# Attention and feed-forward on one core: feed-forward groups of 384 tokens behind three groups of 256, one PSUM bank for the inner units, one set of score operands

## The chip, the cores and the metric

The kernel runs on one core of one Trainium2 chip. A core has a matrix engine (TensorE, here PE, with its weight loads as PEld), VectorE (DVE), ScalarE (ACT), GpSimd (POOL), and SyncE (SP), which here issues every DMA. Work memory is SBUF; matmuls write to PSUM, which has 8 banks, each of 512 float32 numbers for each of 128 partitions. The metric is the device time of one execution in microseconds (us), lower is better.

## The reference

64 heads (8 batches of 8) of causal attention with a decay, each over 576 positions of width 64, then a two-layer feed-forward over all 4608 tokens (512 to 2048 to 512):

```python
scores = scale * q @ k.T;  decay = cum[:, None] - cum[None, :]     # cum = cumsum(log f)
scores = where(causal, -1e9, scores + decay)
attn = softmax(scores);  x = attn @ v                              # per head
x = x.transpose(0, 2, 1, 3).reshape(4608, 512)                     # heads side by side
h = x @ w_in;  g = maximum(0.01 * h, h);  out = g @ w_out
```

## The kernel before, in words

All large products are made with operands that are split in a high and a low part, and a product is the sum of three matmuls: high by high, high by low, low by high. So the feed-forward needs, for each block of 128 inner units and each group of tokens, 4 (pieces of 512 inputs) x 3 = 12 matmuls for `h`, and 3 matmuls for each 128 tokens for the second layer (`o`).

The program has three stages. In the first (about 166 us) the first 256 positions of three batches are attended to ("early" heads, two at a time: tiles `sce`, `ze`, `tre`, `pte`, `ave`), while the weights come in and are split (tiles `wraw`, `wt`, `win_h`, `win_l`, `wout_h`, `wout_l`) by ACT and DVE. These 768 tokens are feed-forward groups 0, 1 and 2. In the second stage 64 tasks, one for each head, run as a pipeline: in the step of task t stand the scores of t (`sc`, into the exponentials `z`), the transposes of t-1 (`tr`, into the high and low parts `ph`, `pl`), the products with the values of t-1 (`av`, added up by ACT's `y` and DVE's `x`), a normalisation for each pair of heads (`rb`), and `split(t+1)`, which makes the score operands of the next task. The third stage is feed-forward alone (from about 1143 us).

A score is two accumulating matmuls, one with operands `s1`, `m1`, one with `s2`, `m2`. `split` makes them: ACT copies q and k (lines 320, 321), POOL subtracts the high part (line 129, a helper) into half of `s1` and half of `m2`, and three DMAs bring half of `s1` and the decay into `s2` and `m2` (lines 322 to 324). Before, there are two buffers of `s1` and `m1`, and two fixed tiles each of `s2` and `m2` (`s2a`, `s2b`, `m2a`, `m2b`) that even and odd tasks use in turn.

The feed-forward is a generator, `ffn`, that is advanced in quanta: between the pieces of a task stands `fill(step)`, which lets some quanta pass. Before, groups are 256 tokens, and a pair of 128-unit blocks is made in one PSUM bank (tag `h`, two banks): quanta are 12 matmuls of the first block, 12 of the second, and then 6 `o` matmuls for each 128 tokens of the pair before. After the second block ACT applies the activation over 512 columns (line 512, tile `g`), and DVE makes the high and low parts `gh` and `gl` (lines 515, 516). Accumulators of the second layer have one bank each, `o0` and `o1`; two banks each belong to tags `sc` and `tr`: 8 in all. A group's inputs `xs` come by one DMA (line 472) when the group before is partly done, and are split by DVE and POOL (lines 477, 129). At the end of a group ACT copies `o` to `ost` (two buffers, line 551) and SP stores it (line 553). The number of quanta of a task follows from the quanta that are ready, at most `MAXQ`, in eighths of it for each `fill`.

A scheduler places the instructions on each engine's queue; an engine works through its queue in that order. The order is the one that the program's rows show below.

```python
step = min(have / (left + SLACK), MAXQ) / 8
```

Of the kernel before, what the change touches and what calls it, by code (L numbers as in the profile page):

```python
# [20 lines left out]
MAXQ = 9  # L21
# [15 lines left out]
def forgetting_attention_ffn(ctx, tc, qT, kT, v4, vr, f, w_in, w_out, out):  # L37
# [18 lines left out]
    NG = NTOK // T  # L56
    NQ = NFC // 2 * (2 + T // P)
# [42 lines left out]
    def warm(n):  # L100

        ps = psum.tile([P, 512], F32, tag="h", name=f"warm_{len(warmed)}")
# [93 lines left out]
    for name, tag, x, to in (("fck", "s1", fc, dec_k), ("fcq", "m1", start, dec_q)):  # L196
        r = one.tile([P, S], F32R, tag=tag, name=name, bufs=2)
# [40 lines left out]
    def early_scores(b, g):  # L238
# [3 lines left out]
        for o in range(2):  # L242
            s = b * HPB + 2 * g + o
            for i in range(2):
# [9 lines left out]
                z = e[c] = one.tile(  # L254
                    [P, n], F32, tag=tag, name=f"ze_{b}_{g}_{c}", bufs=BUFS.get(tag, 1)
                )
# [14 lines left out]
    def early_values(b, g):  # L271
        e = early[b, g]
        out = psum.tile([P, 512], F32, tag="tr", name=f"ave_{b}_{g}")
        for o in range(2):
# [5 lines left out]
            pt = one.tile([P, 3 * P], F32, tag=("z4", "m2a")[o], name=f"pte_{b}_{g}_{o}")  # L280
# [9 lines left out]
        xh, xl = groups[b]  # L290
# [5 lines left out]
    def fix():  # L296

        for x in "ab":
            for w, n in (("s2", 2), ("m2", 4)):
                y = fixed[w + x] = one.tile([P, S], F32R, tag=w + x, name=f"fixed_{w}{x}")  # L300
                nc.gpsimd.memset(y[:D].bitcast(F32), 0.0)
                nc.gpsimd.memset(y[:n].bitcast(F32), 1.0)
            y = fixed["sum" + x] = one.tile([P, NCH, 2], F32, tag="sum" + x, name=f"fixed_sum{x}")
            nc.gpsimd.memset(y, 1.0)
# [5 lines left out]
    def split(t):  # L310
# [157 lines left out]

    def fetch_group(n):
        if n not in groups and n not in staged and (n + 1) * T <= ready[0]:  # L470
            xs = staged[n] = one.tile([P, NCC, T], F32R, tag="b4", name=f"xs_{n}", bufs=B4)
            nc.sync.dma_start(xs.bitcast(F32), xd[:, n * T:(n + 1) * T].rearrange("(c p) t -> p c t", p=P))

    def split_group(n):
        xs = staged[n]
        xh = one.tile([P, NCC, T], F32R, tag="b4", name=f"xh_{n}", bufs=B4)
        nc.vector.tensor_copy(xh, xs.bitcast(F32))
        minus(xs, xs.bitcast(F32), xh.bitcast(F32))
        groups[n] = (xh, xs)

    def ffn():
# [4 lines left out]
        for at, (n, p0, p1) in enumerate(order):  # L486
            while (n + 1) * T > ready[0]:
# [7 lines left out]
            acc = [None, None]  # L495
            for p in range(p0, p1):
# [3 lines left out]
                ph = psum.tile([P, 2, T], F32, tag="h", name=f"h_{n}_{p}")  # L500
                for e in range(2):
                    fs = slice(e * P, (e + 1) * P)
                    for c in range(NCC):
                        for x, (w, xx) in enumerate(((win_h[p], xh), (win_h[p], xl), (win_l[p], xh))):
                            nc.tensor.matmul(  # L505
                                ph[:, e, :], w[:, c, fs], xx[:, c, :],
                                start=(c == 0 and x == 0), stop=(c == NCC - 1 and x == 2),
                            )
# [3 lines left out]
                nc.scalar.activation(g, ph, AF.Prelu, alpha=0.01)  # L512
# [152 lines left out]
```

## Time and profile before

| what | value |
|---|---|
| three runs | 1254.18, 1258.46 (median), 1259.77 us |
| the profiled execution | span 1251.0 us from the first to the last instruction; no other time of it is on record |
| PE busy, weight loads | 1228.7 us (98%), 1079.2 us (86%) |
| DVE, ACT, POOL busy | 739.0, 609.5, 324.7 us |
| granted PE clock | 1.000 of full speed |
| `h` matmuls, 256 columns | 3456 |
| `o` matmuls, 512 columns | 1728 |
| DMA | 102.49 MB, 82 GB/s on average |

How to read the rows: in a group's row stand line, engine, operation, tiles written and read, shapes and count, then busy time and mean duration, then idle time of the engine just before. A timeline row has the start in us from the span's start, the duration, engine, line and tiles; durations of matmuls overlap, since they are pipelined, so a matmul's price is the time from its start to the next one's. A row of the chain of waits has start, length, and what stood there. A row of the waits view has who waited for whom: us in total, times, longest.

### The profile page before, as it was taken

The page shows a single profiled execution, that of the slowest core. Times are in us where ns is not written, and L with a number is a line of the kernel's source. Part 1 is how long each engine was busy: PE and PEld are TensorE (multiplying, and loading weights), DVE is VectorE, ACT ScalarE, POOL GpSimd, SP SyncE. Part 2 cuts the span into 40 slices and gives each one's busy share as a digit, 9 for nine tenths or more (in the row PEclk, how much of TensorE's full clock was granted, in tenths as well). Part 3 has the DMA queues.
Part 4 walks back from the last instruction along what each step waited for, and adds up shares of the span by engine and source line. Part 5 has one row for each costly group of instructions (what it writes and reads, how often), then busy time and mean ns, then how long its engine had stood idle before and what let it go on. Part 6 is the DMA issues. An engine that isn't in the chain of part 4 may idle for free.

```text
span 1251.0 us, 22163 instructions
## 1 busy us (share of the span) xinstructions
PE 1228.7 (98%) x7964; PEld 1079.2 (86%) x7964; DVE 739.0 (59%) x1837; ACT 609.5 (49%) x1447; POOL 324.7 (26%) x348
## 2 busy tenths in 40 slices
PE   9999999999999999999999999999999999999998
PEld 6667888888998898898988889989999988899997
DVE  7888967766665655655556555453444656764211
ACT  6766556664554554554454445343334545552111
POOL 2000063333233433232223222221322333421000
PEclk9999999999999999999999999999999999999999
DMA  6444342333222322223222222121212222221000
GB/s 196 164 156 145 124 117 89 109 90 96 68 85 84 101 68 59 76 64 96 68 84 85 78 58 64 55 79 43 85 51 66 69 85 75 89 61 42 18 17 18
DMA packets 64078, 102.49 MB, mean 82 GB/s; under 512 B 9057, under 2 KB 32145, under 8 KB 63969
## 3 DMA queue, kind: packets, MB, share of 16 engines
q1 hardware_dynamic: 63968, 101.08, 26.6%
q8 instruction: 63, 1.03, 0.3%
q14 instruction: 47, 0.38, 0.1%
HBM read 74.76 MB, written 18.42 MB: 74 GB/s over the span
## 4 chain that ended last, share of the span: by engine, by line
PE 92%; DVE 3%; DMA 2%; ACT 1%; issue 1%; POOL 0%; SPq 0%; ACTq 0%; DVEq 0%; POOLq 0%
PE h L505 32%; PE o L537 30%; PE sc L352 9%; PE av L421 8%; PE tr L379 7%; PE sce L248 2%; DMA xs<-xd 2%; PE warm L105 1%; PE rb L456 1%; PE ave L283 1%; PE sce L249 1%; DVE gh L515 1%; PE tre L277 1%; DVE fixed_vs L330 0%; ACT g L512 0%
## 5 line engine op out<-in xcount | busy, mean ns | idle before, releaser
L505 PE MATMUL h<-xh,win_h 128*128 128x256 f32 x1152 | 330.8, 287 | 0.1
L505 PE MATMUL h<-xh,win_l 128*128 128x256 f32 x1152 | 326.4, 283 | 0.0
L505 PE MATMUL h<-xs,win_h 128*128 128x256 f32 x1024 | 289.4, 283 | 0.0
L537 PE MATMUL o<-wout_h,gh 128*128 128x512 f32 x576 | 232.4, 404 | 0.2 <-DVE gh L515 0.2
L129 POOL TENSOR_TENSOR s<-qraw,s 64x576 fp32r<-64x576 f32 (+1 forms) x64 | 84.7, 1324 | 566.6 <-ACT s L320 532.2
L537 PE MATMUL o<-wout_l,gh 128*128 128x512 f32 x576 | 226.4, 393 | 0.0
L537 PE MATMUL o<-wout_h,gl 128*128 128x512 f32 x576 | 225.8, 394 | 0.0
L505 PEld LDWEIGHTS h<-xh,win_h 128*128 128x128 f32 x1152 | 219.4, 191 | 4.4 <-ACT xh L291 0.2
L505 PEld LDWEIGHTS h<-xh,win_l 128*128 128x128 f32 x1152 | 219.6, 191 | 0.8 <-issue 0.5
L392 ACT CAST ph<-tr 128x128 fp32r<-128x128 f32 (+3 forms) x272 | 120.1, 444 | 167.3 <-PE tr L379 165.8
L505 PEld LDWEIGHTS h<-xs,win_h 128*128 128x128 f32 x1024 | 195.2, 191 | 3.7
L512 ACT ACTIVATE g<-h 128x512 f32<-128x512 f32 x144 | 85.7, 595 | 228.6 <-PE h L505 223.8
L515 DVE CAST gh<-g 128x512 fp32r<-128x512 f32 x144 | 81.6, 567 | 174.8 <-ACT g L512 172.3
L357 DVE CUSTOM_DVE_ANT_0 z<-sc,tri 128x128 f32<-128x128 f32 (+1 forms) x208 | 107.2, 518 | 122.0 <-PE sc L352 122.0
L363 ACT ACTIVATE z<-z,max 128x128 f32<-128x128 f32 (+1 forms) x208 | 122.5, 589 | 72.9 <-DVE max L357 71.2
L394 DVE TENSOR_TENSOR pl<-tr,ph 128x128 fp32r<-128x128 f32 (+3 forms) x272 | 137.1, 508 | 33.3 <-ACT ph L392 33.2
L537 PEld LDWEIGHTS o<-wout_h,gl 128*128 128x128 f32 x576 | 108.3, 188 | 23.9 <-DVE wraw L162 0.2
L352 PE MATMUL sc<-m,s 128*128 128x128 f32 (+2 forms) x336 | 123.3, 372 | 1.8 <-DVE max L357 1.8
L537 PEld LDWEIGHTS o<-wout_h,gh 128*128 128x128 f32 x576 | 108.8, 189 | 16.0 <-DVE gh L515 0.6
L537 PEld LDWEIGHTS o<-wout_l,gh 128*128 128x128 f32 x576 | 108.8, 189 | 15.3 <-issue 0.2
L516 DVE TENSOR_TENSOR gl<-g,gh 128x512 fp32r<-128x512 f32 x144 | 109.6, 761 | 6.3 <-PE sce L248 2.1
L379 PE MATMUL tr<-ident_r,z 128*128 128x128 f32 x568 | 96.3, 273 | 4.3 <-DVE pl L394 3.0
(113 smaller groups left out, 1836.9 us busy)
## 6 DMA issues: line engine op xcount, KB each, us to landing
kraw<-in_kT SPq DMA_DIRECT2D x128, 144.0 KB
qraw<-in_qT SPq DMA_DIRECT2D x80, 144.0 KB
wraw<-in_w_in SPq DMA_DIRECT2D x16, 512.0 KB
wraw<-in_w_out SPq DMA_DIRECT2D x16, 512.0 KB
vm<-in_v SPq DMA_DIRECT2D x32, 256.0 KB
xs<-xd SPq DMA_DIRECT2D x16, 512.0 KB
out<-ost SPq DMA_DIRECT2D x28, 256.0 KB
xd<-x SPq DMA_DIRECT2D x20, 288.0 KB
```

What stands on the lines that cost most here:

```text
L352: nc.tensor.matmul(ps[:m, :b - a], h["s" + w][:, cols], h["m" + w][:, a:b], start=y == 0, stop=y == 1,)
L357: nc.vector.tensor_tensor_reduce(out=z[:, a:b], in0=ps[:m, :b - a], in1=tri[:m, at:at + b - a], scale=-SCALE, scalar=3.0e38 if x == 0 else ...
L363: nc.scalar.activation(z, z, AF.Exp, bias=h["max"][:m, last:last + 1], scale=-1.0, accum_out=fixed["sum" + "ab"[s // 2 % 2]][:m, i, s % 2: ...
L379: nc.tensor.transpose(ps[:, x * m:(x + 1) * m], z[:m, j * P:(j + 1) * P], ident[:m, :m])
L392: nc.scalar.copy(o, src)
L394: nc.vector.tensor_tensor(o, src, hi.bitcast(F32), op=ALU.subtract)
L421: nc.tensor.matmul(ps[:, a - lo:hi - lo], fixed["vs"][:, odd, j, :], h[w][:, at:at + hi - a], start=(n == 0), stop=(n == len(steps) - 1),)
L505: nc.tensor.matmul(ph[:, e, :], w[:, c, fs], xx[:, c, :], start=(c == 0 and x == 0), stop=(c == NCC - 1 and x == 2),)
L512: nc.scalar.activation(g, ph, AF.Prelu, alpha=0.01)
L515: nc.vector.tensor_copy(gh, g)
L516: nc.vector.tensor_tensor(gl, g, gh.bitcast(F32), op=ALU.subtract)
L537: nc.tensor.matmul(acc[k], gg[:, e, ts], w[:, e, :], start=(fc_ == 2 * p0 and x == 0), stop=(fc_ == 2 * p1 - 1 and x == 2),)
```

## The change

- The first three groups keep 256 tokens; the other 3840 tokens make ten groups of 384 in place of fifteen of 256. Matmuls of `h` have 384 columns there.
- A block of 128 inner units is made by itself: 12 matmuls in one bank, then activation and both parts over 256 or 384 columns. Tag `h` has one bank; the freed bank is `o2`, the accumulator of a group's third 128 tokens.
- A quantum is half of a block: 6 `h` matmuls, or half of the `o` matmuls of the block before (3 or 5 and 4). `MAXQ` goes from 9 to 12, the quanta of the late early steps from 8 to 16.
- There is one buffer of `s1` and of `m1`, and one fixed tile of `s2` and of `m2`. The early heads and the transposed early weights take their scratch tiles from these names.
- `ost` keeps two buffers, for three copies at a group's end.

```diff
-MAXQ = 9
+MAXQ = 12
+LATER = 384
-ZE = (("z0", "z1", "z2", "z3"), ("vm", "s2b", "m2b", "s2a"))
-FQ = (0, 0, 0, 0, 0, 8, 8, 8, 8, 8, 8, 8, 8)
-BUFS = dict(s1=2, m1=2, ost=2)
+ZE = (("z0", "z1", "z2", "z3"), ("vm", "s1", "m1", "s2"))
+FQ = (0, 0, 0, 0, 0, 16, 16, 16, 16, 16, 16, 16, 16)
...
-    NG = NTOK // T
-    NQ = NFC // 2 * (2 + T // P)
+    sizes = [T] * NE + [LATER] * ((NTOK - NE * T) // LATER)
+    first = [sum(sizes[:n]) for n in range(len(sizes))]
+    last = [a + m for a, m in zip(first, sizes)]
+    NG = len(sizes)
+    TM = max(sizes)
+    NQ = NFC * 4
...
-        x = "ab"[t % 2]
-        s1 = h["s1"] = one.tile([P, S], F32R, tag="s1", name=f"s1_{t}", bufs=2)
-        m1 = h["m1"] = one.tile([P, S], F32R, tag="m1", name=f"m1_{t}", bufs=2)
-        s2, m2 = h["s2"], h["m2"] = fixed["s2" + x], fixed["m2" + x]
+        s1 = h["s1"] = one.tile([P, S], F32R, tag="s1", name=f"s1_{t}")
+        m1 = h["m1"] = one.tile([P, S], F32R, tag="m1", name=f"m1_{t}")
+        s2, m2 = h["s2"], h["m2"] = fixed["s2"], fixed["m2"]
...
-            for p in range(p0, p1):
+            for f in range(2 * p0, 2 * p1):
+                p, e = divmod(f, 2)
...
-                ph = psum.tile([P, 2, T], F32, tag="h", name=f"h_{n}_{p}")
-                for e in range(2):
-                    fs = slice(e * P, (e + 1) * P)
...
-                    if e == 0:
+                ph = psum.tile([P, 512], F32, tag="h", name=f"h_{n}_{f}", bufs=1)
+                fs = slice(e * P, (e + 1) * P)
+                mms = [
+                    (a[:, c, fs], b[:, c, :w])
+                    for c in range(NCC)
+                    for a, b in ((win_h[p], xh), (win_h[p], xl), (win_l[p], xh))
+                ]
+                for i, (a, b) in enumerate(mms):
+                    if i == len(mms) // 2:
                         yield True
-                g = one.tile([P, 2, T], F32, tag="b2", name=f"g_{n}_{p}", bufs=B2)
-                nc.scalar.activation(g, ph, AF.Prelu, alpha=0.01)
+                    nc.tensor.matmul(ph[:, :w], a, b, start=i == 0, stop=i == len(mms) - 1)
+                g = one.tile([P, TM], F32, tag="b2", name=f"g_{n}_{f}", bufs=B2)
...
+                nc.scalar.activation(g[:, :w], ph[:, :w], AF.Prelu, alpha=0.01)
+                nc.vector.tensor_copy(gh[:, :w], g[:, :w])
...
-    def second(n, p, p0, p1, gh, gl, acc):
-        for k in range(T // P):
+    def second(n, f, p0, p1, gh, gl, acc):
+        p, e = divmod(f, 2)
+        begin, end = f == 2 * p0, f == 2 * p1 - 1
+        nk = sizes[n] // P
+        done = 0
+        for k in range(nk):
...
+                done += 1
+                if done == (3 * nk + 1) // 2:
+                    yield True
```

Three places of the order show what moves.

PE, first stage, the first blocks of group 0 (`h_<block>`; before, a block's number is that of a pair). Before:

```order
L505 MATMUL h_0_614<-xh_163,win_h_93 128x256
L505 MATMUL h_0_614<-xl_164,win_h_93 128x256
L505 MATMUL h_0_614<-xh_163,win_l_101 128x256
L277 MATMUL tre_3_0_528<-ident_r,ze_3_0_408 128x128
L505 MATMUL h_1_645<-xh_163,win_l_102 128x256
L505 MATMUL h_1_645<-xh_163,win_h_94 128x256
L277 MATMUL tre_3_0_528<-ident_r,ze_3_1_417 128x128 x2
L505 MATMUL h_1_645<-xl_164,win_h_94 128x256
```

With the change, two blocks further on in the same stage:

```order
L519 MATMUL h_3_685<-xl_164,win_h_94 128x256
L519 MATMUL h_3_685<-xh_163,win_l_102 128x256
L552 MATMUL o_0_0_652<-wout_h_110,gh_2_674 128x512
L552 MATMUL o_0_0_652<-wout_l_118,gh_2_674 128x512
L552 MATMUL o_1_0_656<-wout_h_110,gh_2_674 128x512
L552 MATMUL o_1_0_656<-wout_l_118,gh_2_674 128x512
L519 MATMUL h_4_710<-xh_163,win_h_95 128x256
```

Before, matmuls of pair 1 stand on PE while pair 0 is still open in the other bank. Now block 4 begins when block 3 is finished, with four `o` matmuls between them, and its first matmul needs the bank that block 3's activation reads.

ACT, second stage, around `split` (`s_22`, `m_22` are the copies for task 22, `z_20` exponentials of task 20; `fixed_z` holds a task's last exponentials). Before:

```order
L363 ACTIVATE z_20_5353,fixed_suma<-z_20_5353,max_5298 128x512
L512 ACTIVATE g_3_5371<-h_3_5333 128x512
L392 CAST ph_5291<-tr_4_5377 128x5x64
L320 CAST s_22_5652<-qraw_5487 128x576
L321 CAST m_22_5653<-kraw_5490 128x576
L363 ACTIVATE fixed_z_1714,fixed_suma<-fixed_z_1714,max_5298 64x576
L428 COPY y_0_5418<-av_0_5407 64x448
```

With the change:

```order
L364 ACTIVATE z_23_5994,fixed_sumb<-z_23_5994,max_5920 128x512
L393 CAST ph_5913<-tr_4_6012 128x5x64
L321 CAST s_24_6078<-qraw_5881 128x576
L322 CAST m_24_6079<-kraw_5884 128x576
L364 ACTIVATE fixed_z_1812,fixed_sumb<-fixed_z_1812,max_5920 64x576
L429 COPY y_0_6048<-av_0_6037 64x448
```

The copies stand at the same place behind a task's scores, but before they are for the task after next, and now for the next one.

ACT, second stage, at the end of a group (`ost_<k>` is the copy of the k-th 128 tokens). With the change (before, there is no third copy):

```order
L525 ACTIVATE g_0_7030<-h_0_6996 128x384
L429 COPY y_1_7039<-av_1_7036 64x128
L568 COPY ost_0_7045<-o_0_0_6000 128x512
L568 COPY ost_1_7074<-o_1_0_6004 128x512
L568 COPY ost_2_7080<-o_2_0_6008 128x512
L525 ACTIVATE g_1_7106<-h_1_7083 128x384
```

The third copy takes the buffer of the first, so it waits for the first store; the next group's activation `g_1` is queued behind it.

More of the change, by code (lines that the diff above doesn't have):

```diff
@@ L196, in forgetting_attention_ffn @@
     for name, tag, x, to in (("fck", "s1", fc, dec_k), ("fcq", "m1", start, dec_q)):
-        r = one.tile([P, S], F32R, tag=tag, name=name, bufs=2)
+        r = one.tile([P, S], F32R, tag=tag, name=name)
         halves(r, x)
@@ L279, in early_values @@
                 )
-            pt = one.tile([P, 3 * P], F32, tag=("z4", "m2a")[o], name=f"pte_{b}_{g}_{o}")
+            pt = one.tile([P, 3 * P], F32, tag=("z4", "m2")[o], name=f"pte_{b}_{g}_{o}")
             nc.scalar.copy(pt, ps[:, :3 * P])
@@ L289, in early_values @@
             return
-        xh, xl = groups[b]
+        xh, xl = (x[:, :, :T] for x in groups[b])
         nc.scalar.copy(xh[:, g, :], out[:, :T])
@@ L296, in fix @@
     def fix():
+        for w, n in (("s2", 2), ("m2", 4)):
+            y = fixed[w] = one.tile([P, S], F32R, tag=w, name=f"fixed_{w}")
+            nc.gpsimd.memset(y[:D].bitcast(F32), 0.0)
+            nc.gpsimd.memset(y[:n].bitcast(F32), 1.0)
         for x in "ab":
[L299 to L302, printed above, removed]
             y = fixed["sum" + x] = one.tile([P, NCH, 2], F32, tag="sum" + x, name=f"fixed_sum{x}")
@@ L467, in forgetting_attention_ffn, with wide @@
     groups, staged = {}, {}
+    def wide(name, n):
+        return one.tile([P, NCC, TM], F32R, tag="b4", name=f"{name}_{n}", bufs=B4)
     def fetch_group(n):
-        if n not in groups and n not in staged and (n + 1) * T <= ready[0]:
-            xs = staged[n] = one.tile([P, NCC, T], F32R, tag="b4", name=f"xs_{n}", bufs=B4)
-            nc.sync.dma_start(xs.bitcast(F32), xd[:, n * T:(n + 1) * T].rearrange("(c p) t -> p c t", p=P))
+        if n not in groups and n not in staged and last[n] <= ready[0]:
+            xs = staged[n] = wide("xs", n)
+            nc.sync.dma_start(
+                xs[:, :, :sizes[n]].bitcast(F32),
+                xd[:, first[n]:last[n]].rearrange("(c p) t -> p c t", p=P),
+            )
     def split_group(n):
[L475 to L478, printed above, removed]
+        xs, xh = staged[n], wide("xh", n)
+        a, b = (x[:, :, :sizes[n]] for x in (xs, xh))
+        nc.vector.tensor_copy(b, a.bitcast(F32))
+        minus(a, a.bitcast(F32), b.bitcast(F32))
         groups[n] = (xh, xs)
@@ L486, in ffn @@
         for at, (n, p0, p1) in enumerate(order):
-            while (n + 1) * T > ready[0]:
+            w = sizes[n]
+            while last[n] > ready[0]:
                 yield False
@@ L519, in ffn @@
                     yield from second(*pending)
-                if p == p1 - 1 and at + 1 < len(order):
+                if e == 1 and p == p1 - 1 and at + 1 < len(order):
                     m = order[at + 1][0]
@@ L544, in second @@
                 nc.scalar.copy(o, acc[k])
-            elif p == p1 - 1:
+            elif end:
                 if (n, k) in parts:
@@ L551, in second @@
                     nc.scalar.copy(o, acc[k])
-                for x, row, m in segments(n * T // P + k):
+                for x, row, m in segments(first[n] // P + k):
                     nc.sync.dma_start(out[row:row + m, :], o[x:x + m])
-            yield True
+        yield True
     parts = {}
@@ L572, in forgetting_attention_ffn @@
     for n in range(2):
-        groups[n] = tuple(
-            one.tile([P, NCC, T], F32R, tag="b4", name=f"{name}_{n}", bufs=B4)
-            for name in ("xh", "xl")
-        )
+        groups[n] = tuple(wide(name, n) for name in ("xh", "xl"))
     TRI = (NFULL + 1) * P
@@ L605, in forgetting_attention_ffn @@
         now = list(range(*tasks[t][1:])) if t < nt else []
-        have = ready[0] // T * NQ - used[0]
+        have = sum(x <= ready[0] for x in last) * NQ - used[0]
         left = min((e + 2 - t for e in ends if e + 1 >= t), default=1)
```

44 lines of the change are left out of this document (18 added, 26 removed).

## The prediction

> **What bounds the kernel now.** I read the page first (busy shares, the chain of waits), then the stages, then single places in the timeline.
>
> ```profile
> PE 1228.7 (98%) x7964; PEld 1079.2 (86%) x7964; DVE 739.0 (59%) x1837; ACT 609.5 (49%) x1447; POOL 324.7 (26%) x348
> PE 92%; DVE 3%; DMA 2%; ACT 1%; issue 1%; POOL 0%; SPq 0%; ACTq 0%; DVEq 0%; POOLq 0%
> ```
>
> PE is busy for 98% of the span and is 92% of the chain. Where PE's queue has no hole, a matmul less is time saved, and a wait more is time lost. The stages differ in who is next:
>
> ```profile
> 120.00:150.00 30.00, 30.00 (x171) 23.36 (x170) 25.51 (x45) 19.50 (x43) 0.98 (x2) 1.00 0.43 140
> sum 166.00, PE 161.16 PEld 119.03 DVE 136.89 ACT 103.55 POOL 18.30; mean PE 26.86 PEld 19.84 DVE 22.81 ACT 17.26 POOL 3.05
> 900.00:1000.00 100.00, 100.00 (x674) 90.60 (x673) 51.72 (x128) 43.06 (x95) 24.35 (x28) 1.00 0.21 62
> ```
>
> The columns are the window, its length, and then busy time of PE, PEld, DVE, ACT and POOL. Over the first 166 us DVE is at 136.89 (82%) and ACT at 103.55: they have little room there. Late in the second stage DVE is at 52% and ACT at 43%.
>
> **The feed-forward matmuls.** What an `h` and an `o` matmul cost PE is read from the chain in the last stage, where they stand back to back:
>
> ```profile
> 1154.36 2.87 PE h L505 x24
> 1157.23 2.75 PE o L537 x12
> 605.83 0.34 PE L352 MATMUL sc<-fixed_m2b,fixed_s2b 128*128 128x384 f32 x1
> 606.01 0.39 PE L537 MATMUL o<-wout_h,gh 128*128 128x512 f32 x1
> ```
>
> 24 matmuls of 256 columns take 2.87 us, 119.6 ns each; 12 of 512 take 2.75 us, 229.2 ns each. The straight line through both is 10.0 ns for each matmul and 0.428 ns for each column, so 384 columns cost 174.4 ns. The one kind of row with 384 columns ahead of another full matmul, a score, agrees within its rounding: 0.18 us from start to start. The counts follow from the groups (192 `h` matmuls each): before 18 x 192 = 3456. Now 3 x 192 = 576 of 256 columns and 10 x 192 = 1920 of 384, so 2880 matmuls of 256 become 1920 of 384: 344.4 us becomes 334.8, **-9.6 us**. Both ends: at the `o` rate for each column, 172 ns, it is -14.4; at the rounded 180 ns it is +1.2. The 174.4 lies on the line, so I take it. The `o` matmuls stay 1728 of 512 columns.
>
> The Trainium skill (TensorE: Matmul & The Clock Gate, "Back-to-back issue gap") gives a warm matmul N/2.4 + 2.5 ns. That would be 109.2 and 162.5 ns here, so by it the fixed part is small and the wider groups would save an estimated 2.4 us. The trace's 119.6 ns speaks against it.
>
> **One bank for `h`.** Now each block's first matmul waits until the activation of the block before has read the bank. What that takes with ACT free:
>
> ```profile
> 1168.19 0.28 PE L505 MATMUL h<-xh,win_l 128*128 128x256 f32 x1
> 1168.56 0.60 ACT L512 ACTIVATE g<-h 128x512 f32<-128x512 f32 x1 [5.02 <-PE h L505]
> ```
>
> The activation ends 0.97 us after the start of the last `h` matmul. With 384 columns it is shorter than with 512. In the order at least nine `o` matmuls (9 x 229.2 ns = 2.06 us) stand between two blocks of 384, so the wait is covered twice over, and nothing is paid as long as ACT is on time. In the first stage the cover is six `o` matmuls of a 256 group (1.37 us), at two places four (0.92 us) and at one a single score matmul, and ACT is not always on time:
>
> ```profile
> 102.08 0.28 PE L505 MATMUL h<-xh,win_l 128*128 128x256 f32 x1
> 103.39 1.16 ACT L150 ACTIVATE wt<-wraw 128x1024 f32<-128x1024 f32 x1 [1.20 <-DVE wraw L162]
> 104.45 0.58 ACT L512 ACTIVATE g<-h 128x512 f32<-128x512 f32 x1
> ```
>
> The block was done at 102.08, and its activation began 2.37 us later, behind a weight pass that itself waited for DVE. Before, PE went on in the other bank. 28 of the blocks stand in this stage. Beside the wait, DVE and ACT have more instructions there, since a pair is now two. The nearest rows:
>
> ```profile
> L392 ACT CAST ph<-tr 128x512 fp32r<-128x512 f32 x64 | 37.5, 586 | 22.8 <-PE tr L379 21.8
> L392 ACT CAST ph<-tr 128x256 fp32r<-128x256 f32 x40 | 14.9, 371 | 10.9 <-PE tr L379 10.7
> L394 DVE TENSOR_TENSOR pl<-tr,ph 128x512 fp32r<-128x512 f32 x64 | 43.9, 685 | 1.3 <-ACT ph L392 1.3
> L394 DVE TENSOR_TENSOR pl<-tr,ph 128x256 fp32r<-128x256 f32 x40 | 16.8, 419 | 1.4 <-ACT ph L392 1.4
> ```
>
> Two of 256 for one of 512 cost DVE 2 x 419 - 685 = 153 ns more, and ACT 2 x 371 - 586 = 156. With two DVE operations and one of ACT for each of 14 pairs that is 4.3 us of DVE and 2.2 of ACT. If all of the stage hangs on DVE, 4.3 us are paid; if PE alone sets it, nothing. DVE is 82% busy and PE 97%, so I take a third, **+1.5 us**. Gain from this I exclude: nothing is taken off either engine. After the first stage the same operations cost no path: ten groups of 16 blocks of 384 take ACT no more than the 595 ns for each pair did, and it is at 43%.
>
> **One set of score operands.** The copies for a task must now wait for the scores of the task just before it. What then must pass until its first scores:
>
> ```profile
> 610.72 0.29 PE L352 MATMUL sc<-fixed_m2b,fixed_s2b 128*64 128x288 f32 x1
> 610.96 0.67 ACT L320 CAST s<-qraw 128x576 fp32r<-128x576 f32 x1 [0.16 <-PE sc L352]
> 613.21 1.43 POOL L129 TENSOR_TENSOR fixed_m2b<-kraw,m 64x576 fp32r<-64x576 f32 x1
> 612.28 0.86 PE L421 MATMUL av<-ph,fixed_vs 128*128 128x448 f32 x5
> 613.74 0.47 PE L537 MATMUL o<-wout_h,gh 128*128 128x512 f32 x1
> 615.21 0.22 PE L421 MATMUL av<-ph,fixed_vs 128*128 128x128 f32 x1
> 615.38 0.45 PE L537 MATMUL o<-wout_h,gh 128*128 128x512 f32 x1
> ```
>
> From the last score (610.72) to the end of POOL's last part (614.64) pass 3.92 us; before, that is hidden behind a whole task, some 17 us. Queued behind ACT's copy are the last exponentials and `y`, as before. The shortest cover in the new order is from task 7 to 8: three `o` (0.69 us), ten `av` (1.46, from 612.28 to 613.74), two more (0.17, from 615.21 to 615.38), twelve `h` of 256 (1.44), one transpose (0.11): 3.87 us and the last score's own 0.14. So it just holds, and tasks 1 to 8 have 3.9 to 5.1. From task 17 on the `h` and `o` between are 7 us and more. From task 0 to 1 the two matmuls of a score are set apart, and the one with `m2` stands 4.5 us behind. Late cases come where POOL is still at a group's split:
>
> ```profile
> L129 POOL TENSOR_TENSOR xs<-xs,xh 128x1024 fp32r<-128x1024 f32 x16 | 38.4, 2399 | 84.2 <-DVE xh L477 84.0
> ```
>
> It grows by half, to 3.6 us, but comes 11 times in place of 16. I take **+0.5 us**; the ends are 0 and 8 (each of eight early tasks late by 1 us).
>
> **The end of a group.** Two buffers serve three copies. At the end of the program:
>
> ```profile
> 1245.67 0.59 ACT L551 COPY ost<-o 128x512 f32<-128x512 f32 x1 [3.46 <-PE o L537]
> 1246.29 1.69 SPq L553 DMA_DIRECT2D out<-ost  x2
> 1247.03 0.58 ACT L551 COPY ost<-o 128x512 f32<-128x512 f32 x1 [0.77 <-PE o L537]
> SPq L661 <- DMA out<-ost: 1.5, 2, 1.3
> ```
>
> The last copy ends at 1247.61; SP's second issue ends at 1247.98, and then SP waits 1.5 us for the landings, so a store lands about 2.0 us after its copy. Let E be the end of PE's work. The first copy starts at E - 1.37 (six `o` before the end) and ends at E - 0.78, its store lands at E + 1.2, and the third copy ends at E + 1.8 in place of E + 0.6: **+1.2 us** (0 if the store is done in 0.8, 2.5 if it takes the 3.4 us from 1247.61 to the span's end). At the other group ends ACT stands still for up to the same 1.2 us with the next activation behind it. PE needs that one only after twelve `h` and nine `o` more; from the first copy's start to the bank's next use the order has 1.37 + 2.09 + 2.06 = 5.5 us at the least, against 0.6 + 2.0 + 0.6 + 0.6 = 3.8. Covered; it costs if SP's issue is 1.7 us late.
>
> **Late groups.** Where a group's input comes late, DVE's queue stands behind it, then ACT's exponentials, then the activation:
>
> ```profile
> 567.82 0.29 PE L505 MATMUL h<-xh,win_l 128*128 128x256 f32 x1
> 569.82 0.69 DVE L477 CAST xh<-xs 128x1024 fp32r<-128x1024 f32 x1 [5.32 <-DMA xs<-xd]
> 571.36 0.58 ACT L512 ACTIVATE g<-h 128x512 f32<-128x512 f32 x1
> DVE xh L477 <- DMA xs<-xd: 20.2, 10, 5.3
> ```
>
> Here the activation was 3.54 us late. With one bank 2.06 of that would be covered, so some 1.5 us would be new. DVE's waits of this kind are 20.2 us in ten; most are short, and there are fewer groups. I take half a case, **+0.7 us** (0 to 5).
>
> **Sum:** -9.6 + 1.5 + 0.5 + 1.2 + 0.7 = -5.7 us. Against the profiled span that is 1251.0 to 1245.3. The median of the runs is 7.5 us above that span and the fastest 3.2; as a difference on the median it gives 1252.8, so I say **1253 us**. Changes under 0.5%, 6.3 us, can hardly be told from none here: faster is under 1252.2, slower over 1264.8.
>
> **The rivals.** *PE's holes close as well (faster).* Quanta are now 1.04 us pieces in place of 1.4, and the order lays them between steps that stood together:
>
> ```profile
> PE rb L456 <- DVE x L429: 6.5, 9, 1.4
> ```
>
> At 7 of 32 normalisations `rb` followed the last `av` at once; now at none. If these 6.5 us go, the time is 1252.8 - 6.5 = 1246, say 1247. Against it: finer pieces are also thinner covers.
>
> *The single bank in the first stage (slower).* If each of the 27 changes of block there meets ACT in a weight pass (1.16 us) and loses half of it, 0.58, on top of the cover, that is 15.7 us, and the time is 1268. It decides from 0.45 us for each change of block (12 us). For it: ACT is 62% busy there (103.55 of 166), and the row of 104.45. Against it: most of ACT's idle time there waits for PE, and there are `o` matmuls to cover.
>
> *The fixed part of a matmul is small (no change).* If 10.0 ns is the price of 256 columns alone, and 384 cost 180, the saving is gone and the costs of 3.9 us and the +1.2 remain: 1263 at worst, and 1260 with the fixed part at 2.5 ns (960 x 2.5 = 2.4 saved). The skill's rule is of this kind. Against it: 119.6 and 229.2 lie on one line with the score's 0.18.
>
> *The costs cancel the gain (no change).* If DVE sets the first stage (+4.3) and the late groups cost their upper 5: 1258.5 - 9.6 + 4.3 + 0.5 + 1.2 + 5 = 1260; about 1258 with half of it.
>
> **How the numbers follow.** The forecast has 0.50, with a range of its own of 1249 to 1257; two fifths of that (0.20) lie under 1252.2. Closed holes 0.20, the single bank 0.17, the small fixed part 0.06, the cancelled gain 0.07. So faster 0.20 + 0.20 = 0.40, no change 0.30 + 0.06 + 0.07 = 0.43, slower 0.17. The range from 1246 to 1265 leaves out some of the fastest case and most of the slow one.
>
> **What would show it.** The first scores of a task now begin here:
>
> ```profile
> 167.99 0.22 PE L352 MATMUL sc<-m,s 128*128 128x128 f32 x1
> ```
>
> With the change, in the last stage twelve `h` of 384 columns take 2.09 us in the chain (2.16 would be the 180 ns) and nine `o` 2.06, with no hole between. In the first stage PE's waits for ACT's activation stay under 3 us in sum, and the first scores come within 2 us of 167.99; 10 us later would be the single bank. PE's waits for POOL or DMA ahead of `sc` stay under 1 us in sum. The last three copies show the third one waiting about 1 us for a DMA. The forecast is wrong if PE's idle time grows by more than 6 us, or if `h` of 384 costs more than 178 ns.

## The result

| kernel | time (median) | ratio to before, 95% interval |
|---|---|---|
| before | 1257.6 us | 1 |
| the change | 1272.7 us | 1.0117 [1.0078, 1.0156] |

The change is slower by 1.2%, about 15 us; the prediction was 1253 us with a range of 1246 to 1265. The execution that was profiled first took three times as long throughout (4094 us), so the profile after is that of a second profiled execution, e1 below: span 1269.9 us, 18.9 more than before.

Part of any difference between two executions here is the granted clock. Beside e1, the kernel before has spans of 1249.6 to 1251.0 us at a clock of 1.000 and of 1259.1 to 1260.6 at 0.990. The change has 1264.1 and 1265.0 at 0.997, where the kernel before has 1253.2 to 1254.4 (beside e9 and e13). So at the same clock the change is 10 to 12 us behind. The rest of the 15 goes with a clock that is lower more often: its middle execution is at 0.991, that of the kernel before, beside e1, at 0.995. Where "at one clock" stands below, it is an estimate: a straight line through the spans of all executions but the outliers gives 1.06 us for each 0.001 of clock, and each kernel is compared on that line with the kernel before beside it, to about 1 us. What a wait costs by bringing the clock down is left out of it.

The page of the change, busy time and engines' shares of the chain:

```profile
PE 1233.6 (97%) x7004; PEld 1070.9 (84%) x7004; DVE 774.6 (61%) x1960; ACT 613.2 (48%) x1511; POOL 316.6 (25%) x339
PE 83%; DVE 6%; DMA 4%; issue 3%; ACT 2%; POOL 1%; SPq 0%; DVEq 0%; ACTq 0%; POOLq 0%
```

PE has 960 matmuls less, and its idle time is 1269.9 - 1233.6 = 36.3 us in place of 22.3, 14 us more; the prediction had named 6 as the sign of being wrong. DVE's share of the chain doubled. Where that lies, in windows cut at the stages and around one stretch of the first (length, then busy time of PE, PEld, DVE, ACT, POOL, then the granted clock). Before:

```profile
47.00:61.00 14.00, 13.35 (x75) 9.62 (x75) 11.86 (x25) 10.29 (x27) 0.00 (x0) 1.00 0.33 121
168.00:350.00 182.00, 176.69 (x1185) 156.01 (x1184) 126.00 (x350) 109.33 (x279) 70.53 (x72) 1.00 0.32 95
350.00:1130.00 780.00, 771.90 (x5183) 696.47 (x5182) 445.71 (x1162) 377.82 (x894) 230.56 (x242) 1.00 0.24 72
1130.00:1251.00 121.00, 117.00 (x746) 106.04 (x744) 29.33 (x56) 18.75 (x35) 5.30 (x3) 1.00 0.07 24
```

After:

```profile
47.00:61.00 14.00, 13.54 (x43) 8.89 (x44) 9.21 (x23) 7.30 (x19) 0.00 (x0) 0.52 0.46 157
178.00:350.00 172.00, 158.75 (x1031) 138.69 (x1030) 133.39 (x364) 104.29 (x286) 64.27 (x66) 1.00 0.31 90
350.00:1161.00 811.00, 800.55 (x4588) 715.65 (x4588) 471.32 (x1239) 385.78 (x937) 233.52 (x246) 0.99 0.25 72
1161.00:1269.90 108.90, 102.98 (x530) 92.78 (x527) 28.48 (x60) 18.01 (x37) 4.01 (x2) 0.99 0.07 24
```

The last stage is 12 us shorter, in part because work moved: PE is busy 14 us less in it and 11 us more in the second. The first is 10 us longer, with a stretch of 14 us at half clock in it. The second is 983 us in place of 962, and PE stands idle in it for (172 - 158.75) + (811 - 800.55) = 23.7 us, before for 13.4. PE's waits in the change (who for whom, us in total, times, longest):

```profile
PE rb L457 <- DVE x L430: 10.5, 7, 3.1
PE av L422 <- DVE pl L395: 5.7, 5, 2.4
PE tr L380 <- DVE x L430: 3.1, 3, 2.2
PE sc L353 <- POOL fixed_m L133: 0.3, 1, 0.3
PE h L519 <- ACT g L525: 0.2, 1, 0.2
```

What the prediction feared, waits for the single `h` bank and for POOL's operands, comes to 0.5 us. What grew are waits for DVE. The timeline at the longest of them:

```profile
720.38 3.44 POOL L133 TENSOR_TENSOR xs<-xs,xh 128x1536 fp32r<-128x1536 f32 x1
720.55 3.69 DVE L527 TENSOR_TENSOR gl<-g,gh 128x384 fp32r<-128x384 f32 x1
721.34 0.60 PE L457 MATMUL rb<-ident_r,rw 128*128 128x128 f32 x4
724.59 0.29 DVE L430 TENSOR_TENSOR x<-av,y 64x128 f32<-64x128 f32 x1
725.03 0.30 PE L457 MATMUL rb<-ident_r,rw 128*128 128x128 f32 x1 [3.10 <-DVE x L430]
726.65 0.52 PE L519 MATMUL h<-xs,win_h 128*128 128x384 f32 x1
```

DVE's subtraction `gl`, 674 ns on average, takes 3.69 us here: it starts 0.17 us after POOL's long subtraction and ends 0.42 us after it, as if it had waited for POOL's end and then run. The small `x` behind it on DVE is late, `rb` waits for `x`, PE stands still for 3.10 us, and then its matmuls start 0.32 us apart (726.65 to 726.97) in place of 0.175: half clock, for 3.4 us. I call such a lengthened DVE instruction a hold. There is one at 403 (a cast of `gh`, 2.66 us, and behind it `gl`, 1.65 us beside POOL's subtraction of an operand) and one at 974 (`gl`, 3.22 us). There PE waits 1.92 and 2.42 us for `pl`, which stands behind them on DVE, and 3.4 us at half clock follow as well.

### The profile page after: what moved, and what is told of

It is laid out like the page before. It is cut to its first block, busy times and chain, and to the rows that moved or that the text cites. A ratio compares the mean times of both kernels' runs of the same rounds, so it can differ in the third digit from the quotient of the medians.

```text
span 4094.2 us, 20486 instructions
## 1 busy us (share of the span) xinstructions
PE 4086.7 (100%) x7004; PEld 2631.1 (64%) x7004; DVE 716.7 (18%) x1960; ACT 635.4 (16%) x1511; POOL 306.1 (7%) x339
## 4 chain that ended last, share of the span: by engine, by line
PE 100%; ACT 0%; issue 0%; DVE 0%; ACTq 0%
PE h L519 35%; PE o L552 35%; PE sc L353 9%; PE av L422 8%; PE tr L380 7%; PE sce L252 2%; PE rb L457 1%; PE warm L109 1%; PE ave L285 1%; PE tre L279 1%; PE ave L286 0%; PE sce L253 0%; ACT pte L283 0%; ACT xh L293 0%; ACT ost L568 0%
## 5 line engine op out<-in xcount | busy, mean ns | idle before, releaser
L519 PE MATMUL h<-xh,win_h 128*128 128x384 f32 (+1 forms) x832 | 711.2, 855 | 1.1 <-ACT xh L293 0.9
L519 PE MATMUL h<-xh,win_l 128*128 128x384 f32 (+1 forms) x832 | 694.8, 835 | 0.0
L552 PE MATMUL o<-wout_h,gh 128*128 128x512 f32 x576 | 633.7, 1101 | 0.0
L552 PE MATMUL o<-wout_h,gl 128*128 128x512 f32 x576 | 628.3, 1096 | 0.0
L552 PE MATMUL o<-wout_l,gh 128*128 128x512 f32 x576 | 625.4, 1086 | 0.0
L519 PE MATMUL h<-xs,win_h 128*128 128x384 f32 (+1 forms) x704 | 614.4, 873 | 0.0
L519 PEld LDWEIGHTS h<-xh,win_h 128*128 128x128 f32 x832 | 367.8, 442 | 146.4 <-issue 109.8
L519 PEld LDWEIGHTS h<-xh,win_l 128*128 128x128 f32 x832 | 378.9, 455 | 108.9 <-issue 87.9
L519 PEld LDWEIGHTS h<-xs,win_h 128*128 128x128 f32 x704 | 313.4, 445 | 123.5 <-issue 105.9
L525 ACT ACTIVATE g<-h 128x384 f32<-128x384 f32 (+1 forms) x208 | 96.9, 466 | 1422.0 <-PE h L519 1383.3
L353 PE MATMUL sc<-m,s 128*128 128x128 f32 (+2 forms) x336 | 304.7, 908 | 0.0
L380 PE MATMUL tr<-ident_r,z 128*128 128x128 f32 x568 | 288.2, 692 | 0.0
L353 PE MATMUL sc<-fixed_m,fixed_s 128*128 128x128 f32 (+2 forms) x336 | 264.3, 787 | 0.0
```

What stands on the lines that cost most here:

```text
L353: nc.tensor.matmul(ps[:m, :b - a], h["s" + w][:, cols], h["m" + w][:, a:b], start=y == 0, stop=y == 1,)
L380: nc.tensor.transpose(ps[:, x * m:(x + 1) * m], z[:m, j * P:(j + 1) * P], ident[:m, :m])
L519: nc.tensor.matmul(ph[:, :w], a, b, start=i == 0, stop=i == len(mms) - 1)
L525: nc.scalar.activation(g[:, :w], ph[:, :w], AF.Prelu, alpha=0.01)
L552: nc.tensor.matmul(acc[k], gg[:, ts], w[:, e, :], start=begin and x == 0, stop=end and x == 2)
```

## The experiments

All ratios are to the kernel before, timed beside each.

**Undoing parts of the change.** Three theories stood at first: the clock (the stretches at half clock are the loss), the first stage (the single bank), and the second stage (thinner covers, that is, less other work for PE between the pieces of a task). e1 is the change itself. e2 makes all groups 256, e3 gives `h` its two banks back on top of e2, e4 is the kernel before with one set of score operands.

```diff
-MAXQ = 12                      # e2
-LATER = 384
+MAXQ = 18
+LATER = 256
-... tag="h", ..., bufs=1)      # e3: e2, and both tiles of the tag
+... tag="h", ..., bufs=2)
-s2, m2 = fixed["s2" + x], fixed["m2" + x]   # e4: from before; likewise s1, m1 and ZE
+s2, m2 = fixed["s2"], fixed["m2"]
```

> The change as it is, again. Its first profile ran every TensorE row about three times slower than the kernel before and its fast runs had a mean granted clock of 0.985 to 0.997, against 1.000 in the profile of before. Theory clock: the wider, denser stream is granted less than the full clock for parts of the run; then time follows the granted clock run by run (about 0.8 us for each 0.001), and the profile shows windows with a clock under 1.00. Theory first stage (the single bank): the clock is 1.00 in the profile and the first scores begin 8 to 15 us later than the 167.99 of before. Theory second stage (thin covers): the first scores are on time, and TensorE's idle time after 170 us is 10 us or more above that of before.

> The change with all groups at 256 tokens (MAXQ 18 in place of 12, so that a task still gets about 12.5 us of feed-forward): blocks one by one in one bank and one set of operands stay, the wider matmuls go. Theory clock (wider matmuls draw more): back near the time of before, clock 1.000, within 4 us of 1257.6. Theory single bank or thin covers: as slow as the change or slower, since the 9.6 us of matmul overhead come back: 1275 to 1285.

> As the run before, with two banks for the inner units (the third accumulator's bank is free at 256 tokens). The order of instructions is the same, so only the wait for the bank differs. Theory single bank: 10 to 15 us faster than with one bank. Theory clock and theory thin covers: within 3 us of it.

> The kernel before with one set of score operands alone (single buffers of s1, m1, s2, m2; the early scratch tiles renamed as in the change). If the operands' cover holds as the prediction says: within 3 us of before. If the cover does not hold: 5 to 10 us slower, with TensorE waiting ahead of the score matmuls in tasks 1 to 10.

| run | median | ratio, 95% interval |
|---|---|---|
| e1 | 1271.1 | 1.0109 [1.0077, 1.0141] |
| e2 | 1267.1 | 1.0067 [1.0041, 1.0093] |
| e3 | 1271.5 | 1.0113 [1.0046, 1.0179] |
| e4 | 1255.5 | 0.9991 [0.9958, 1.0023] |

Two banks do not help (e3 is no faster than e2), so the single bank is not the cause; e2's wait of `h` for the activation is `PE h L519 <- ACT g L525: 2.0, 2, 1.8`. One set of operands costs nothing that can be measured, though PE waits 2.5 us for POOL ahead of `sc` in e4's trace. Most of the loss is there already with groups of 256, made block by block. e2 fits none of the ranges that I gave for it: the theory of the clock had it within 4 us of 1257.6, the other two at 1275 to 1285.

**POOL's hold, the first stage's clock, the early groups.** e5 cuts POOL's subtraction of a group in four; e6 adds twelve matmuls that are to keep PE busy from 40 to 60 us; e7 makes six early groups of 256; e8 is all three.

```diff
-        minus(a, a.bitcast(F32), b.bitcast(F32))            # e5
+        for c in range(NCC):
+            minus(a[:, c], a[:, c].bitcast(F32), b[:, c].bitcast(F32))
+                elif b == 1 and g < 3:                      # e6
+                    ps = psum.tile([P, 512], F32, tag="o2", ..., bufs=1)
+                    nc.tensor.matmul(ps[:, :T], ident, x0[:, 0, :], start=True, stop=True)
-    sizes = [T] * NE + [LATER] * ...                        # e7
+    sizes = [T] * (2 * NE) + [LATER] * ...
```

> The change, with POOL's subtraction that splits a staged group cut from one instruction (128x1536, 3.44 to 3.51 us, 2.4 us at 1024 before) into four of 128x384. Theory hold: the one long subtraction holds a VectorE cast or subtraction that starts beside it until it ends (3.69, 3.22 and 2.66 us for instructions of some 0.5), the TensorE holes of 3.26, 2.59 and 2.08 us at 722, 976 and 406 follow, and each brings 3.4 us at half clock; all three holes and stretches go, up to 7.9 + 5.1 = 13 us, so 1258 to 1265 us against 1271. Theory first stage (the change's loss is the 10 us by which the first scores come later): the time stays at 1268 to 1273. Theory starvation (the larger groups leave too little feed-forward work behind the first tasks): the same, 1268 to 1273.

> The change, with twelve more matmuls whose results nobody reads (four behind the scores of each of the first three pairs of heads of the second batch, into the third output bank, which is free there). Theory first stage: the hole of 1.6 us before 46.9 brings 13.7 us at half clock (46.8 to 60.5), about 6.9 us; with TensorE kept busy the clock stays whole there, the first scores come at 170 to 174 instead of 178.15, and the time falls by 4 to 8 us, to 1263 to 1267. If the stage is bound by ScalarE and VectorE and the half clock only fills their waits, the first scores stay within 2 us of 178 and the time at 1269 to 1273. Theory hold and theory starvation: no change but for the matmuls added, 1269 to 1274.

> The change, with six groups of 256 tokens ahead of eight of 384 instead of three ahead of ten. The h matmuls of the 768 tokens that go back to 256 columns cost 6 x 192 x (59.8 - 58.1) ns = 2 us more. Theory starvation: a group of 384 can start only when its last token is there, so there is less feed-forward work to lay behind the first tasks (TensorE stalls of 21.2 us from 150 to 350 us against 11.2 before); with smaller groups there 5 to 10 us of it go, so 1263 to 1268. Theory hold: one of the three holes (406 us) goes or shrinks, the two later ones stay: 1268 to 1272. Theory first stage: 1271 to 1274.

> The three edits together. If all three theories hold and their losses add up, 1271 - 10 - 6 - 4 = 1251 us, 1246 to 1256, below the kernel before (1256.5). If only one is right: that one's gain, 1258 to 1268. If the stalls move elsewhere, with the work behind them just as thin: above 1265.

| run | median | ratio, 95% interval |
|---|---|---|
| e5 | 1261.6 | 1.0040 [1.0004, 1.0077] |
| e6 | 1279.6 | 1.0173 [1.0135, 1.0211] |
| e7 | 1267.0 | 1.0088 [1.0058, 1.0118] |
| e8 | 1256.9 | 1.0003 [0.9971, 1.0035] |

The hold is real: e5 takes 9.5 us off the median, 8.7 by the ratios. The same place in it:

```profile
716.40 4.25 POOL L133 TENSOR_TENSOR xs<-xs,xh 128x384 fp32r<-128x384 f32 x4
716.58 1.25 DVE L528 TENSOR_TENSOR gl<-g,gh 128x384 fp32r<-128x384 f32 x1
719.30 0.30 PE L457 MATMUL rb<-ident_r,rw 128*128 128x128 f32 x1 [1.35 <-DVE x L430]
```

POOL takes longer in all (4.25 us), but `gl` gets in between two pieces, and PE waits 1.35 us, without a stretch at half clock. The three stretches after 400 us are gone; two of 3.4 us stand at new places (300 and 1075 us), behind holes in PE's work of 2.90 and 1.81 us. e7 shows the early groups: the windows of the `h` and then the `o` matmuls alone between 250 and 350 us (length, busy time of PE, of PEld), of the kernel before, of the change, and of e7:

```profile
250.00:350.00 100.00, 35.53 (x263) 33.22 (x264) 1.00 0.30 87
250.00:350.00 100.00, 31.91 (x122) 21.57 (x120) 1.00 0.30 87
```

```profile
250.00:350.00 100.00, 28.80 (x168) 25.56 (x168) 1.00 0.32 92
250.00:350.00 100.00, 28.83 (x99) 16.63 (x100) 1.00 0.32 92
```

```profile
250.00:350.00 100.00, 33.67 (x235) 30.97 (x234) 1.00 0.31 91
250.00:350.00 100.00, 33.53 (x117) 20.11 (x117) 1.00 0.31 91
```

Before, 67 us of PE time is feed-forward there, in the change 58, in e7 67 again: a group of 384 is usable only when its last token is, so less stands ready to cover the tasks. e7 alone is 4 us faster than the change by the medians, 2.6 by the ratios, which is within the intervals.

e6 is 8 us slower than the change, above every range that I gave: the remedy failed. It has 24 more matmul records, and its one trace is of its slowest execution, with half-clock stretches at other places, so it doesn't tell what the stretch at 47 us is worth. Other traces do. Up to the first scores e1, e5, e7, and e9 and e14 below have the same 862 matmuls on PE in the same order. With 13.7 us at half clock the first scores come at 178.15, 177.68 and 177.58 (e1, e5, e9), without at 172.91 and 172.97 (e7, e14). So the stretch costs about 5 us there. It is not the change's alone: the traces of e4 and e10, which are the kernel before but for one edit each, have 23.9 and 10.2 us at half clock in their first stage. e8 is level with the kernel before in spite of e6's matmuls.

**Which holds, and the order block by block.** e9 is pieces and six early groups without e6's matmuls; e10 puts the pieces into the kernel before, as a control; e11 is e9 with more matmuls at the program's start; e12 is e2 with pieces.

```diff
-WARM = (20, 2)                                              # e11
+WARM = (28, 2)
-        minus(xs, xs.bitcast(F32), xh.bitcast(F32))         # e10, in the kernel before
+        for c in range(NCC):
+            minus(xs[:, c], xs[:, c].bitcast(F32), xh[:, c].bitcast(F32))
```

> The change with POOL's split in four pieces and six early groups of 256, without the added matmuls. Theory hold and theory starvation, as separate losses: 1271 - 9.5 - 4 = 1257.5 us. The run with all three edits had a second stage of 963.2 us against 974.4 with the pieces alone, and its twelve added matmuls (24 on TensorE) and its first stage cost some 6: without them 1250 to 1254, below the kernel before. If the two losses are the same holes counted twice: 1260 to 1263.

> The kernel before, with POOL's subtraction of a staged group (128x1024, 2.4 us) in four of 128x256. Theory hold: there the long subtraction hits TensorE at few places (holes of 1.53 and 1.27 us at 429 and 706), so 1 to 4 us are gained: 1253 to 1257 against 1257.6. If the hold costs the kernel before as much as the change (9.5), it is no cause of the difference between them: 1248.

> As the run with pieces and six early groups, and 28 instead of 20 matmuls on zeros at the program's start. Theory first stage: TensorE runs dry at about 11 us, where the first decay operands come, and in some executions that brings 24 us at half clock (14.9 to 38.8, seen in three profiles); eight more matmuls (8 x 0.23 us) cover it. So 2 to 5 us less than without them in the median, and a narrower spread. If the half clock there does not hang on this hole: the same median within 2 us.

> All groups of 256 tokens, made block by block in one bank, with POOL's subtraction in four of 128x256 (without that 1267.1). Theory hold: the subtraction is 2.4 us there as in the kernel before, and only one hole follows it (450.5, 1.95 us, with 3.4 us at half clock), so 2 to 5 us are gained: 1262 to 1265; what is left against the kernel before (some 6 to 8 us) is then of the order block by block: four waits of rb for x of 1.1 to 1.7 us from 208 to 280, one of tr of 2.4, the first stage. If all of it comes from the hold: 1257 to 1259.

| run | median | ratio, 95% interval |
|---|---|---|
| e9 | 1255.1 | 0.9952 [0.9922, 0.9982] |
| e10 | 1251.7 | 0.9955 [0.9919, 0.9992] |
| e11 | 1263.2 | 1.0022 [0.9997, 1.0047] |
| e12 | 1257.2 | 0.9980 [0.9953, 1.0006] |

The kernel before gains from the pieces too, 0.45% or 5.7 us; I expected 1 to 4, and the change gains 8.7. Its own trace shows why: a cast of `gh`, 567 ns on average, beside POOL's 2.38 us.

```profile
289.05 2.38 POOL L129 TENSOR_TENSOR xs<-xs,xh 128x1024 fp32r<-128x1024 f32 x1 [3.19 <-DVE xh L477]
289.23 2.49 DVE L515 CAST gh<-g 128x512 fp32r<-128x512 f32 x1
```

e12 gains 10 us over e2, where the subtraction is no longer than before; I expected 2 to 5. But the control gains as well: with pieces in both, the order block by block (e12) is still behind the kernel before (e10), by 3.1 us in the ratios, whose intervals overlap, and 5.7 at one clock; without pieces (e2) it is 8.4 and 9.3. So POOL's subtraction of a group accounts for about half of what that order costs at 256 tokens, and the rest is something else. e11 is 8 us behind e9, 4.5 of it at one clock; all its executions have a clock of 0.985 to 0.992. More matmuls early do not raise the clock here, and why is open.

**The waits of `rb`.** In e1, e2, e5, e7, e9 and e12 `rb` waits 0.9 to 1.5 us four times between 200 and 282 us. At the first of these places in the change:

```profile
207.01 1.44 POOL L133 TENSOR_TENSOR fixed_m<-kraw,m 64x576 fp32r<-64x576 f32 x1
207.10 1.40 DVE L333 CAST fixed_vs<-vt 64x64 fp32r<-64x64 f32 x1 [0.61 <-POOL s L133]
208.74 0.63 DVE L430 TENSOR_TENSOR x<-av,y 64x448 f32<-64x448 f32 x1
209.51 0.63 PE L457 MATMUL rb<-ident_r,rw 128*128 128x128 f32 x4 [1.52 <-DVE x L430]
```

A cast of 64 columns takes 1.40 us beside POOL's operand subtraction of 1.44. Three theories for these waits: too short a lead, the time from a block to its `o` matmuls (e13: e12 with two blocks pending, eight `b2` buffers); too little cover ahead of `rb` (e14: e9 with a fill moved there); POOL (e15: e9 with the operand subtractions cut in three; e16 is the control, both cuts in the kernel before). e17 is the change with nothing but both cuts; e18 is e15 with e14's cover. The edits, written short:

```diff
-                if pending is not None:                     # e13
-                    yield from second(*pending)
+                if len(pending) == 2:
+                    yield from second(*pending.pop(0))
-                fill(step)                                  # e14, in the values of a task
+                fill(step * (2 if end else 1))              # end: the last part of a pair of heads
-        minus(s1[:D, a:n], ...)                             # e15, e16, e17; m2 likewise
+        for x in range(a, n, 192):
+            minus(s1[:D, x:min(x + 192, n)], ...)
```

> All groups of 256 with pieces (1257.2 us, 1252 at whole clock), and the second matmuls of a block two blocks behind it instead of one. Theory lead (a block's parts must be there after 12 h matmuls, 1.43 us, where a pair's had 24, 2.87): with two blocks the lead is that of the kernel before, TensorE's stalls of the second stage fall by 3 to 6 us, and the time to 1251 to 1254. Theory POOL at rb or theory cover at rb: within 2 us of 1257.

> As the run with pieces and six early groups (1255.1), with one fill of quanta moved from behind a normalisation to ahead of it. Theory cover at rb (too little stands between the last av and rb): the four waits from 200 to 280 us shrink by 0.7 us each and others with them, 2 to 4 us in all: 1251 to 1253. If VectorE's lateness there comes from POOL, the cover helps as well but less (TensorE still waits where the quantum is short): 1253 to 1255. If the cover is missed elsewhere: 1255 to 1258.

> As the run with pieces and six early groups (1255.1), with POOL's two operand subtractions of a task (64x576, 1.43 us) in three of 192 columns each. Theory POOL at rb (at 207.10 a VectorE cast of 64x64 takes 1.40 us beside POOL's 1.44, then x is late, then rb waits 1.52): the holds fall to some 0.5 us, the waits of rb by two thirds, 4 to 7 us over the second stage: 1248 to 1251. Theory cover at rb or lead: 1254 to 1257.

> The kernel before with POOL's group subtraction in four (1251.7) and its operand subtractions in three. Theory POOL at rb: rb waits 6.5 us in the kernel before as well, so 1 to 4 us are gained: 1248 to 1251. If only the order block by block is sensitive to it: 1251 to 1253.

> The change itself (three early groups), with POOL's group subtraction in four and its operand subtractions in three. Theory POOL alone (all that the prediction missed in the second stage is VectorE held by POOL): the same as with six early groups, 1247 to 1250, and 5 us or more below the kernel before, as the prediction's sum had it. Theory starvation (three groups are too few, whatever POOL does): 4 to 6 us behind the run with six, 1251 to 1254.

> Six early groups, all of POOL's long subtractions in pieces, and the fill of quanta ahead of rb. If cover and pieces remove the same waits (rb's waits are 1.0 us with the pieces, of 6.0): 1246 to 1249, no better than with the pieces alone (1247.6). If the cover helps elsewhere: 1242 to 1245.

| run | median | ratio, 95% interval |
|---|---|---|
| e13 | 1255.7 | 0.9989 [0.9966, 1.0012] |
| e14 | 1250.0 | 0.9949 [0.9923, 0.9976] |
| e15 | 1247.6 | 0.9917 [0.9892, 0.9942] |
| e16 | 1254.8 | 0.9988 [0.9961, 1.0016] |
| e17 | 1251.3 | 0.9961 [0.9933, 0.9989] |
| e18 | 1245.5 | 0.9896 [0.9854, 0.9938] |

The lead falls: e13 is where e12 is. The cover of e14 leaves the ratio of e9 as it was; at one clock it gains 2.6 us, and the waits of `rb` fall from 6.0 to 4.1 us, so cover plays a small part. The larger part is POOL: the waits of `rb` in e9, and then in e15,

```profile
PE rb L457 <- DVE x L430: 6.0, 7, 1.5
```

```profile
PE rb L462 <- DVE x L435: 1.0, 3, 0.3
```

go from 6.0 to 1.0 us, and the ratio from 0.9952 to 0.9917. The small cast in the change and in e15 (shortest, median and longest of 64, ns):

```profile
L333 DVE CAST fixed_vs<-vt x64: 132/180/1443, 164.8 to 1151.5; 64x64 fp32r<-64x64 f32 x64
```

```profile
L338 DVE CAST fixed_vs<-vt x64: 175/508/994, 172.5 to 1134.9; 64x64 fp32r<-64x64 f32 x64
```

The cast is held more often in e15 (the median grew), but for less: it is the longest hold that costs. In the kernel before, the operand pieces add nothing that can be seen (e16 to e10: 0.9988 and 0.9955, the intervals overlap), against both ranges that I gave for e16.

e17 gives the account of the change: 1.0109 as it is, 1.0040 with the group's subtraction in pieces, 0.9961 with the operands' too. That is 8.7 and 9.9 us of 1257, 18.6 in all. In the kernel before the first cut alone brings 5.7 us (e10) and both together 1.5 (e16); at one clock it is 3.4 for each of the two. So 13 to 17 us of the 18.6 are the change's own, 12 at one clock. Why the operands' hold costs so much in the change and nothing in the kernel before, no run separates: the order block by block and the single set of operands are both candidates.

e17 is not where POOL alone would have put it (1247 to 1250). Six early groups take off 5.5 us more (e15), 2.9 at one clock; the other two pairs of this kind, e1 to e7 and e5 to e9, give 2.6 and 11.1, so the size is uncertain. e18 is the fastest kernel of this study, 1.0% ahead of the kernel before; over e15 its cover gains 2.6 us, which is within the intervals.

## Why the prediction was wrong

**The matmuls were right.** The chain in the last stage of the change:

```profile
1255.68 2.08 PE o L552 x9
1257.76 2.10 PE h L519 x12
1263.84 2.40 DMA out<-ost
1266.34 0.58 ACT ost L568
```

Twelve `h` take 2.10 us (predicted 2.09), nine `o` 2.08 (2.06): 175.0 ns for each `h`, so 2880 x 119.6 - 1920 x 175.0 = 8.4 us are saved of the 9.6. The rival of a small fixed part falls: it needed 180 ns. The Trainium skill (TensorE: Matmul & The Clock Gate, "Back-to-back issue gap") gives N / 2.4 + 2.5 ns for the isolated gap, and says itself that a stream with weight loads differs; its 162.5 ns is 12.5 below the row.

**One bank for `h`** was right as to waits: 0.2 us for the activation, and e3 shows that a second bank gains nothing. The slower rival named this bank and had its time nearly right (1268) by luck, for the wrong reason. The size of the first stage was wrong: +1.5 was predicted. In e7, whose clock stayed whole until 413 us, the first scores start at

```profile
172.91 0.22 PE L353 MATMUL sc<-m,s 128*128 128x128 f32 x1
```

4.9 us later than before, and beyond the upper end that I gave (4.3, all of the stage on DVE). The other 5.2 of the 10.2 in e1 (178.15) are its 13.7 us at half clock.

**One set of score operands.** Its own price was right: e4 gives nothing, and in e1 PE waits 0.3 us for POOL ahead of `sc`. But here lies the step that failed. I wrote of POOL's split that it "grows by half, to 3.6 us, but comes 11 times in place of 16", and priced it only as a delay in POOL's own queue. The row is as I said,

```profile
L133 POOL TENSOR_TENSOR xs<-xs,xh 128x1536 fp32r<-128x1536 f32 x10 | 35.3, 3529 | 88.6 <-DVE xh L484 88.5
```

but for as long as it runs, it can hold a DVE instruction that starts beside it, and who waits for DVE was not asked. The sum put this wait at nothing: it took PE's waits for DVE in the second stage as unchanged. They were not. The runs show two holds in its place, a longer one from the group's subtraction and one from the operands' subtraction, whose length (1.44 us) did not change: cutting both gives back 18.6 us in the change and 1.5 to 5.7 in the kernel before. The row of 289.23 in the profile of before showed such a hold, 2.49 us in place of 0.57.

The Trainium skill (SBUF — State Buffer, "Who interferes with whom") has the rule: VectorE and GpSimd share a pair of ports, and where a GpSimd instruction that reads SBUF has them, a VectorE instruction with two SBUF inputs, or a cast in a two-port mode, is blocked for the whole instruction. The traces agree for both kinds: `gl` with two inputs 3.69 us beside POOL's 3.44, the cast 1.40 beside 1.44. In which mode the cast ran they do not show.

**Late groups** (+0.7): right to be small. DVE's wait for `xs` fell from 20.2 to 10.0 us, `h` did not wait. What the larger groups do cost is another thing, of which the prediction has no term: less feed-forward work behind the first tasks, 5.5 us (e17 to e15), with the doubt given there.

**The end** (+1.2): right in kind, too small. The first two copies stand together, and the third waits 2.40 us for a store, which lands 3.0 us after the first copy's end (1263.25 to 1266.24) and not 2.0. The last matmul, before and after:

```profile
1246.61 0.39 PE L537 MATMUL o<-wout_h,gl 128*128 128x512 f32 x1
1263.60 0.39 PE L552 MATMUL o<-wout_h,gl 128*128 128x512 f32 x1
```

From its start to the end of the span pass 4.4 us before and 6.3 after: +1.9.

**PE's holes close** (the faster rival): the opposite came. `rb` waits 10.5 us for DVE, before 6.5. What spoke against it, that finer pieces are thinner covers, fits the runs, but only together with POOL: with both cuts these waits nearly go (1.0 us in e15).

So the sum of -5.7 was right in its largest term; it left out POOL's hold and the early groups, and had the first stage too small. With the hold cut out the change is 0.4% below the kernel before, 4.9 us. Against the kernel before with cuts it is between 3.4 us ahead (e16, both cuts) and 0.8 behind (e10, the first cut alone); at one clock it is 2.6 ahead of either. By that estimate about half of the -5.7 is left.

## What to carry to other kernels

Before lengthening a POOL instruction, look in the trace for DVE instructions that take several times their mean and end with a POOL one; each is a hold, and its price is what PE waits for behind it. Try POOL's two-input instructions in pieces of some 0.6 to 1 us: here they took longer in all, and cost less where PE waited behind a hold (the operand pieces gained 9.9 us in the change and nothing in the kernel before). Put such a cut into the kernel before as well, as a control: without e10 and e16 all 18.6 us would have been charged to the change. When the order of the work is made finer, re-price the waits that the coarse pieces covered, even on engines that the change doesn't touch; and before making pieces of work larger, count how much of it is ready at the stage that lives on it.

## What the hardware showed beyond that

In the change, holes in PE's work of 1.92, 3.10 and 2.42 us (at 406, 722 and 976 us) were each followed by 3.4 us at half clock, but one of 2.22 us at 294 was not. A hole of 1.33 us at 45.6, between sparse matmuls, was followed by 13.7 us, and the same hole in e7 and e14 (1.30 and 1.33 us) by none. So the length of a hole alone does not decide it. The half-clock stretches inside the traces have lengths of 3.4, 6.8, 10.2, 13.7, 17.1, 20.5, 23.9 and 37.5 us, all multiples of 3.41. The Trainium skill (TensorE: Matmul & The Clock Gate, "Part 1: The HAM clock gate") has a free-running window of about 3.4 us after whose idleness the clock halves; the lengths agree, but here holes shorter than the window were enough. Beside e9 the kernel before runs, but for two outliers, at clocks from 1.000 down to 0.987, with spans from 1248.0 to 1264.8 us. In the change, neither more matmuls at the start (e11) nor in the middle of the first stage (e6) kept the clock up, and both were slower.
